# One-token attention with a gated MLP: five 32 KB slots and straight-line programs replaced by three 64 KB slots and a loop on each engine

## The chip, the core and the metric

The kernel runs on one core of a Trainium2 chip. The core's engines are TensorE (PE, matmuls; PEld is its weight load), VectorE (DVE), ScalarE (ACT), GpSimd (POOL) and SyncE (SP), which issues the transfers here; 16 DMA engines move data between HBM and the core's memory. The metric is the device time of one execution in microseconds, the median of several runs.

## The reference

For two rows of x (D = 448) the kernel computes one step of attention over a cache (16 heads of 256, 4096 cached positions), a ReLU MLP (1792 wide), and mixes the two by a sigmoid gate. All data is float32.

```python
q = (x @ wq).reshape(B, Sq, H, Dh)                      # B=2, Sq=1, H=16, Dh=256
scores = einsum("bhqd,bhkd->bhqk", q, k_cache) * Dh ** -0.5   # 4096 positions
o = einsum("bhqk,bhkd->bhqd", softmax(scores), v_cache)
a = o.reshape(B, Sq, H * Dh) @ wo
b = relu(x @ w1) @ w2
g = sigmoid((x * gate_w).sum(-1))
return g * a + (1 - g) * b
```

Keys and values are 134 MB each, the weights 21 MB. Each byte is used for one or two rows of x only.

## The kernel before

The work is cut into 32 units, one for each head and batch row (`U = 32`). A unit has 4 MB of keys (`kt[u]`, 128 partitions by 32 KB) and 4 MB of values (`vt[u]`). Each is one transfer of 128 rows of 32 KB into one of five slots of a ring (`SLOTS = 5`, `load`, L55), all of them issued by SP in program order. SP waits, before a transfer, until the slot's former content is used.

For each unit, `scores` runs 16 matmuls (32 passes in the trace, since each float32 matmul is two) on PE into one of two PSUM tiles `ps` (L153), DVE takes the maximum (L156), ACT the exponential with its sum (L158); `values` runs 8 products of the value slot with the probabilities on DVE, each with a running sum (L164). Positions are spread over four groups of 32 partitions; `combine` joins them with matmuls (L173 to L199), once for the first 16 units, in the middle of the program, and once for the last 16, at the end.

The query (`make_q`, L122 to L129) and the gate (`make_gate`) come first; x arrives in a small transfer of its own, issued by ACT. The hidden layer of the MLP (`hidden`, L211 to L224) runs in the middle, after unit 17. At the end come `mlp_out` (L238, 14 matmuls into `acc`) and the projection by `wo`: 26 of 32 slices into `acc` (L244), a copy (`a_sb`, L251), a matmul by `fold` that joins the four groups into `z` (L254), the last 6 slices straight into `z` (L258), the copy to `res` (L261) and the transfer of the result (L262). The second half of `wo` is loaded in four parts (L58):

```python
    CUTS = (0, NO - 10, NO - 6, NO - 2, NO)
    TAIL = 6
```

The order of the instructions on each engine is the order in which the code above is written out; the framework adds waits for buffers and data, and closes with a wait for all transfers, a barrier of all engines, the clearing of the semaphores and a second barrier (these stand under L342).

Of the kernel before, what the change touches and what calls it, by code (L numbers as in the profile page):

```python
# [1 line left out]

# [9 lines left out]
AX = mybir.AxisListType  # L12

P, HP = 128, 64
G = 4
R = P // G
SLOTS = 5
NB = 2


@with_exitstack
def tile_gated_mix_decode(ctx: ExitStack, tc: tile.TileContext, xg, kt, vt, wq, wo, w1, w2, out):
    nc = tc.nc
    U, _, T, S = kt.shape
    J, SG = vt.shape[2], vt.shape[3]
    KC, B = xg.shape[1], xg.shape[2] - 1
    KF = KC - 1
    NF, D = w2.shape[1], w2.shape[2]
    DG = D // G
    FG = NF * P // G  # L30
    H = U // B
    DH = T * P
    RB = R // B
    HB = H // NB
    UB = U // NB
    HH = HB // G
    CW = 512
    SCALE = float(DH) ** -0.5

    const = ctx.enter_context(tc.tile_pool(name="const", bufs=1))  # L40
    ring = ctx.enter_context(tc.tile_pool(name="ring", bufs=SLOTS))
    work = ctx.enter_context(tc.tile_pool(name="work", bufs=2))
    ps_s = ctx.enter_context(tc.tile_pool(name="ps_s", bufs=2, space=bass.MemoryType.PSUM))
    ps_w = ctx.enter_context(tc.tile_pool(name="ps_w", bufs=3, space=bass.MemoryType.PSUM))
    ps_a = ctx.enter_context(tc.tile_pool(name="ps_a", bufs=1, space=bass.MemoryType.PSUM))
    ctx.enter_context(tc.manual_schedule())

    def load(src, shape, cuts=None):
        t = ring.tile([P, T * S], F32, name="slot")
        n = 1  # L50
        for s in shape[1:]:
            n *= s
        flat = t[:, :n]
        if cuts is None:
            nc.sync.dma_start(flat, src)  # L55
        else:
            for lo, hi in zip(cuts, cuts[1:]):
                nc.sync.dma_start(flat[:, lo:hi], src[:, lo:hi])  # L58
        return t

    def psum(name="pw"):
        return ps_w.tile([P, CW], F32, name="pw")

    xg_sb = const.tile([P, KC, B + 1], F32, name="xg_sb")
    nc.scalar.dma_start(xg_sb, xg)
    wq_t = [load(wq[i], (P, wq.shape[2])) for i in range(NB)]

    ident = const.tile([P, P], F32, name="ident")
    make_identity(nc, ident)


    sel = const.tile([P, R], F32, name="sel")
    nc.vector.tensor_reduce(sel, ident.rearrange("p (g r) -> p r g", g=G), axis=AX.X, op=ALU.add)
    fsum = const.tile([P, B], F32, name="fsum")
    nc.vector.tensor_reduce(fsum, sel.rearrange("p (b r) -> p b r", b=B), axis=AX.X, op=ALU.add)
    fold = const.tile([P, B, RB], F32, name="fold")
    nc.vector.tensor_scalar(fold, fsum[:, :, None].to_broadcast([P, B, RB]), 1.0 / RB, None, op0=ALU.mult)


    xr = const.tile([P, KC, B, RB], F32, name="xr")  # L80
    nc.vector.tensor_copy(xr, xg_sb[:, :, :B, None].to_broadcast([P, KC, B, RB]))  # L81
    xu = const.tile([P, KC, UB // B, B], F32, name="xu")
    nc.vector.tensor_copy(xu, xg_sb[:, :, None, :B].to_broadcast([P, KC, UB // B, B]))

# [3 lines left out]
    def flat(a):  # L88
        return a.rearrange("p b r -> p (b r)")


    omg = const.tile([P, 1], F32, name="omg")
    gu = const.tile([UB, 1], F32, name="gu")

    def make_gate():
        pg = psum()
        for g in range(G):
            for c in range(KC):
                r = rows_of(c)
                nc.tensor.matmul(pg[g * R:(g + 1) * R, :1], flat(xr[r, c]), xg_sb[r, c, B:], start=(c == 0),  # L100
                                 stop=(c == KC - 1))
        gp = const.tile([P, 1], F32, name="gp")
        nc.scalar.activation(gp, pg[:, :1], AF.Sigmoid)
        nc.vector.tensor_scalar(omg, gp, -1.0, 1.0, op0=ALU.mult, op1=ALU.add)
        pu = psum()
        for c in range(KC):
            r = rows_of(c)
            nc.tensor.matmul(pu[:UB, :1], flat(xu[r, c]), xg_sb[r, c, B:], start=(c == 0), stop=(c == KC - 1))
        nc.scalar.activation(gu, pu[:UB, :1], AF.Sigmoid)


    qt = [const.tile([P, 2, T, G, B], F32, name=f"qt{i}") for i in range(NB)]
    W = 2 * KF * DH

    def make_q(i):
        pq = psum()
        w = wq_t[i]
        for c in range(KC):
            for g in range(G):
                r = rows_of(c, g // 2)  # L120
                at = g * W + c * CW if c < KF else G * W + g % 2 * CW
                nc.tensor.matmul(pq[g * R:(g + 1) * R, :], flat(xr[r, c]), w[r, at:at + CW], start=(c == 0),  # L122
                                 stop=(c == KC - 1))
        q = work.tile([P, CW], F32, name="q", bufs=1)
        nc.scalar.activation(q, pq, AF.Copy, scale=SCALE)
        pt = psum()
        for k in range(2 * T):
            nc.tensor.transpose(pt[:, k * P:(k + 1) * P], q[:, k * P:(k + 1) * P], ident)
        nc.scalar.activation(qt[i].rearrange("p s t g b -> p (s t g b)"), pt[:, ::RB], AF.Copy)  # L129

    nm = [const.tile([P, UB], F32, name=f"nm{i}") for i in range(NB)]
    ls = [const.tile([P, UB], F32, name=f"ls{i}") for i in range(NB)]
    ov = [const.tile([P, UB, J], F32, name=f"ov{i}") for i in range(NB)]
    junk = const.tile([P, SG], F32, name="junk")

    def place(u):
        h, b = divmod(u, B)
        i, hl = divmod(h, HB)  # L140
        hh, hq = divmod(hl, G)
        return i, (hq * HH + hh) * B + b

    def scores(u, k):
        h, b = divmod(u, B)
        i, at = place(u)
        hp, s = divmod(h % HB, 2)
        ps = ps_s.tile([P, SG], F32, name="ps")
        for c in range(SG // CW):
            for t in range(T):  # L150
                for g in range(G):
                    lo = t * S + g * SG + c * CW
                    nc.tensor.matmul(ps[g * R:(g + 1) * R, c * CW:(c + 1) * CW],  # L153
                                     qt[i][:, s, t, hp, b:b + 1].to_broadcast([P, R]), k[:, lo:lo + CW],
                                     start=(t == 0), stop=(t == T - 1))
        nc.vector.tensor_reduce(nm[i][:, at:at + 1], ps, axis=AX.X, op=ALU.max, negate=True)  # L156
        p = work.tile([P, SG], F32, name="p")
        nc.scalar.activation(p, ps, AF.Exp, bias=nm[i][:, at:at + 1], accum_out=ls[i][:, at:at + 1])  # L158
        return p

    def values(u, p, v):
        i, at = place(u)
        for j in range(J):
            nc.vector.scalar_tensor_tensor(junk, v[:, j * SG:(j + 1) * SG], 1.0, p, op0=ALU.mult, op1=ALU.mult,  # L164
                                           accum_out=ov[i][:, at, j:j + 1])

    acc = ps_a.tile([P, D], F32, name="acc")

    def combine(i):
        tp = psum()
        nc.tensor.transpose(tp[:UB, :P], nm[i], ident)  # L173
        nc.tensor.transpose(tp[:UB, P:2 * P], ls[i], ident)  # L174
        mt = tp[:UB, 0:P:R]
        lt = tp[:UB, P:2 * P:R]
        nb = work.tile([UB, 1], F32, name="nb")
        nc.vector.tensor_reduce(nb, mt, axis=AX.X, op=ALU.min)  # L178
        e = work.tile([UB, G], F32, name="e")
        nc.scalar.activation(e, mt, AF.Exp, bias=nb, scale=-1.0)  # L180
        el = work.tile([UB, G], F32, name="el")
        lsum = work.tile([UB, 1], F32, name="lsum")
        nc.vector.scalar_tensor_tensor(el, e, 1.0, lt, op0=ALU.mult, op1=ALU.mult, accum_out=lsum)
        rl = work.tile([UB, 1], F32, name="rl")
        nc.vector.reciprocal(rl, lsum)
        wb = work.tile([UB, G, R], F32, name="wb")
        nc.vector.tensor_scalar(wb, e[:, :, None].to_broadcast([UB, G, R]), rl, gu, op0=ALU.mult, op1=ALU.mult)  # L187
        wp = psum()
        nc.tensor.matmul(wp[:, :UB], wb.rearrange("u g r -> u (g r)"), ident[:UB, :UB], start=True, stop=True)  # L189
        os = work.tile([P, UB, J], F32, name="os", bufs=1)  # L190
        nc.vector.tensor_tensor(os, ov[i], wp[:, :UB, None].to_broadcast([P, UB, J]), op=ALU.mult)  # L191
        po = psum()
        n = HH * B * J
# [34 lines left out]

    NO = HH * J
    CUTS = (0, NO - 10, NO - 6, NO - 2, NO)
    TAIL = 6

# [112 lines left out]
```

## Time and profile before

| | us |
|---|---|
| median of three runs | 681.37 (681.27 to 681.67) |
| span of the profiled execution | 679.7 |
| DVE busy | 360.3 (53% of the span) |
| PE busy | 218.5 (32%) |
| ACT busy | 45.0 (7%) |

The span runs from the first instruction to the last; the profiled execution's own time is not printed beside its span, so that the median of the runs, 1.67 us above it, stands for it. The run has 289.55 MB of data transfers. The profile's rows give for each engine what it did, what it waited for, and how long; the windows query gives for any stretch the busy time of each engine, the share of time in which the 16 DMA engines were busy (1.00 is all of them) and the rate in GB/s.

### The profile page before, as it was taken

How to read it: one execution, taken by the hardware profiler on the slowest of the kernel's cores; microseconds unless marked ns; L12 is line 12 of the kernel's file. 1: busy time of each engine (PE TensorE's matmuls, PEld its weight loads, DVE VectorE, ACT ScalarE, POOL GpSimd, SP SyncE). 2: the span in 40 equal slices, each digit the busy share in tenths (PEclk: the TensorE clock that was granted, in tenths of full speed). 3: DMA queues.
4: the chain of work that ended last, by engine and by line, in shares of the span. 5: the costliest groups of instructions: out<-in, count | busy, mean ns of one | idle time of the engine just before them, and what ended most of it. 6: DMA issues, size and time to landing. Idle time of an engine off the chain costs nothing.

```text
span 679.7 us, 3604 instructions
## 1 busy us (share of the span) xinstructions
PE 218.5 (32%) x1335; PEld 58.7 (9%) x1335; DVE 360.3 (53%) x568; ACT 45.0 (7%) x78; POOL 0.7 (0%) x6
## 2 busy tenths in 40 slices
PE   2613333331223323322233152333322233333236
PEld 1100000000000000000000010000000000000002
DVE  0065555656655546566552738555656655556561
ACT  0100000000000000000000010000000000000000
POOL 0000000000000000000000000000000000000000
PEclk9876776656677676556765587666556676665568
DMA  9999999999999999999999999999999999999995
GB/s 377 429 434 432 434 437 434 432 434 434 435 434 432 434 431 432 432 432 432 431 435 433 429 431 434 432 432 433 432 434 432 434 433 432 432 436 435 436 421 236
DMA packets 10689, 289.77 MB, mean 426 GB/s; under 512 B 1328, under 2 KB 1328, under 8 KB 1712
## 3 DMA queue, kind: packets, MB, share of 16 engines
q1 hardware_dynamic: 10528, 289.55, 98.9%
q8 instruction: 10, 0.16, 0.1%
q14 instruction: 7, 0.06, 0.0%
q10 hardware_dynamic: 144, 0.01, 0.0%
HBM read 289.54 MB, written 0.00 MB: 426 GB/s over the span
## 4 chain that ended last, share of the span: by engine, by line
DMA 81%; DVE 11%; PE 7%; issue 0%; SPq 0%; ACT 0%; DVEq 0%
DMA slot<-in_vt 42%; DMA slot<-in_kt 33%; DVE junk L164 10%; DMA slot<-in_wo 6%; PE ps L153 5%; PE acc L244 1%; PE pw L211 1%; SPq L55 0%; PE pw L258 0%; DVE a_sb L251 0%; PE pw L189 0%; PE pw L254 0%; DVE wb L187 0%; PE pw L195 0%; DVE os L191 0%
## 5 line engine op out<-in xcount | busy, mean ns | idle before, releaser
L164 DVE SCALAR_TENSOR_TENSOR junk<-slot,p 128x1024 f32<-128x1024 f32 x256 | 313.5, 1225 | 88.5 <-DMA slot<-in_vt 79.4
L153 PE MATMUL ps<-slot,qt 128*32 128x512 f32 x1024 | 183.3, 881 | 414.6 <-DMA slot<-in_kt 414.6
L156 DVE TENSOR_REDUCE nm<-ps 128x1 f32<-128x1024 f32 x32 | 39.2, 1224 | 199.5 <-PE ps L153 199.5
L153 PEld LDWEIGHTS ps<-slot,qt 128*32 128x32 f32 x1024 | 45.6, 154 | 550.9 <-issue 524.4
L158 ACT ACTIVATE p<-ps,nm 128x1024 f32<-128x1024 f32 x32 | 35.6, 1113 | 562.0 <-DVE nm L156 562.0
L164 DVE DVE_READ_ACCUMULATOR junk<-slot,p 128x1 f32 x256 | 20.8, 81 | 0.0
L238 PE MATMUL acc<-slot,hr 128*32 128x448 f32 x28 | 5.6, 912 | 10.9 <-DMA slot<-in_w 10.9
L122 PE MATMUL pw<-slot,xr 128*32 128x512 f32 (+1 forms) x64 | 9.0, 700 | 0.0
L244 PE MATMUL acc<-slot,ot 128*32 128x448 f32 x52 | 7.1, 680 | 0.2 <-DMA slot<-in_wo 0.2
L100 PE MATMUL pw<-xg_sb,xr 128*32 128x1 f32 (+1 forms) x32 | 2.5, 196 | 12.6 <-DVE xr L81 12.6
L158 ACT ACTIVATION_READ_ACCUMULATOR p<-ps,nm 128x1 f32 x32 | 6.2, 193 | 0.0
L189 PE MATMUL pw<-ident,wb 16*128 16x16 f32 x4 | 1.0, 324 | 15.7 <-DVE wb L187 15.7
L81 DVE COPY xr<-xg_sb 128x128 f32<-128x128 f32 x1 | 0.2, 227 | 10.2 <-DMA xg_sb<-in_xg 10.2
L211 PE MATMUL pw<-slot,xr 128*32 128x448 f32 (+1 forms) x32 | 5.1, 782 | 0.0
L251 DVE COPY a_sb<-acc 128x448 f32<-128x448 f32 x1 | 0.6, 625 | 6.5 <-PE acc L244 6.5
L100 PEld LDWEIGHTS pw<-xg_sb,xr 128*32 128x32 f32 (+1 forms) x32 | 2.3, 147 | 12.7 <-DVE xr L81 12.6
L238 PEld LDWEIGHTS acc<-slot,hr 128*32 128x32 f32 x28 | 1.4, 166 | 15.2 <-DMA slot<-in_w 11.8
L244 PEld LDWEIGHTS acc<-slot,ot 128*32 128x32 f32 x52 | 2.0, 135 | 4.6 <-issue 4.1
L122 PEld LDWEIGHTS pw<-slot,xr 128*32 128x32 f32 (+1 forms) x64 | 1.9, 125 | 5.5 <-issue 5.5
L180 ACT ACTIVATE e<-pw,nb 16x4 f32<-16x4 f32 x2 | 0.5, 254 | 25.7 <-DVE nb L178 25.7
L189 PEld LDWEIGHTS pw<-ident,wb 16*128 16x128 f32 x4 | 0.8, 245 | 16.3 <-DVE wb L187 16.3
L178 DVE TENSOR_REDUCE nb<-pw 16x1 f32<-16x4 f32 x2 | 0.3, 148 | 3.3 <-PE pw L174 3.3
(46 smaller groups left out, 23.0 us busy)
## 6 DMA issues: line engine op xcount, KB each, us to landing
slot<-in_kt SPq DMA_DIRECT2D x32, 4096.0 KB, 38.2
slot<-in_vt SPq DMA_DIRECT2D x32, 4096.0 KB, 42.2
slot<-in_wq SPq DMA_DIRECT2D x2, 3584.0 KB, 11.3
slot<-in_w SPq DMA_DIRECT2D x2, 3136.0 KB, 36.4
slot<-in_wo SPq DMA_DIRECT2D x1, 3584.0 KB, 39.7
slot<-in_wo SPq DMA_DIRECT2D x2, 896.0 KB, 31.7
slot<-in_wo SPq DMA_DIRECT2D x1, 1344.0 KB, 29.2
slot<-in_wo SPq DMA_DIRECT2D x1, 448.0 KB, 33.1
```

The source lines that it names most:

```text
L100: nc.tensor.matmul(pg[g * R:(g + 1) * R, :1], flat(xr[r, c]), xg_sb[r, c, B:], start=(c == 0), stop=(c == KC - 1))
L122: nc.tensor.matmul(pq[g * R:(g + 1) * R, :], flat(xr[r, c]), w[r, at:at + CW], start=(c == 0), stop=(c == KC - 1))
L153: nc.tensor.matmul(ps[g * R:(g + 1) * R, c * CW:(c + 1) * CW], qt[i][:, s, t, hp, b:b + 1].to_broadcast([P, R]), k[:, lo:lo + CW], start=( ...
L156: nc.vector.tensor_reduce(nm[i][:, at:at + 1], ps, axis=AX.X, op=ALU.max, negate=True)
L158: nc.scalar.activation(p, ps, AF.Exp, bias=nm[i][:, at:at + 1], accum_out=ls[i][:, at:at + 1])
L164: nc.vector.scalar_tensor_tensor(junk, v[:, j * SG:(j + 1) * SG], 1.0, p, op0=ALU.mult, op1=ALU.mult, accum_out=ov[i][:, at, j:j + 1])
L180: nc.scalar.activation(e, mt, AF.Exp, bias=nb, scale=-1.0)
L189: nc.tensor.matmul(wp[:, :UB], wb.rearrange("u g r -> u (g r)"), ident[:UB, :UB], start=True, stop=True)
L211: nc.tensor.matmul(ph[g * R:(g + 1) * R, :FG], flat(xr[r, c]), w[r, at:at + FG], start=(c == 0), stop=(c == KC - 1))
L238: nc.tensor.matmul(acc[g * R:(g + 1) * R, :], hr[:, k, :], w[:, k * D:(k + 1) * D], start=(k < G), stop=False)
L244: nc.tensor.matmul(acc[g * R:(g + 1) * R, :], flat(ot[:, k // J, k % J]), w[:, k * D:(k + 1) * D], start=False, stop=(stop and k >= hi - G))
L251: nc.vector.tensor_copy(a_sb, acc)
```

## The change

The kernel is written anew without the framework, with its own semaphores.

- The program of each engine loops: PE, DVE and ACT run ten turns of three units each and two units behind the loop; SP runs nine turns of three transfers, with the transfers of the first and last units outside. A turn's waits compare semaphores with register values, and DVE, ACT and SP compute addresses in registers. No barrier stands in a loop.
- Keys and values of a unit are one array `kv`, 128 rows of 64 KB, one transfer into one of three slots of 64 KB. The last unit is split into keys and values. A slot comes free when DVE has done the unit's eight products (`freed`). These write over the values in place; there is no `junk` tile.
- One PSUM tile `sc` for the scores where there were two; PE starts a unit when ACT has done the exponential of the one before and has copied the unit's query (`queried`).
- x and the gate's weights ride in the rows of `wq`, which is one transfer; w1 and w2 are one transfer `wm` behind the last unit; `wo` is six transfers of 14, 9, 4, 2, 2 and 1 slices behind that.
- One `combine` for all 32 units. It and the hidden layer run at the end, behind `wm`, mixed with the 14 matmuls of the MLP's second layer. 23 slices of `wo` go into `acc`, 9 straight into `z`.
- The gate uses the exponential where there was a sigmoid. It is applied in `wb`, as before.
- The closing barrier and the clearing of the semaphores do not wait for the result's transfer; SP then waits for it and clears its semaphore.

```diff
-SLOTS = 5
-NB = 2
+SLOTS = 3
+CW = 512
+ACC = (14, 9)
+DIRECT = (4, 2, 2, 1)
+FOLD_AT = 1
...
+    slot = [nc.alloc_sbuf_tensor_at(f"slot{i}", [P, SW], F32, offset=first + i * SW * 4).ap() for i in range(SLOTS)]
...
+    sp.dma_start(slot[0][:, :wq.shape[1]], wq).then_inc(slot_in[0], 16)
+    sp.dma_start(slot[1], kv[0]).then_inc(slot_in[1], 16)
+    sp.dma_start(slot[2], kv[1]).then_inc(slot_in[2], 16)
...
+    def unit_pe(k, u_wait, slot_wait, s):
+        pe.wait_ge(slot_in[s], slot_wait)
+        pe.wait_ge(queried, u_wait)
         for c in range(SG // CW):
             for t in range(T):
                 for g in range(G):
                     lo = t * S + g * SG + c * CW
+                    m = pe.matmul(sc[g * R:(g + 1) * R, c * CW:(c + 1) * CW],
+                                  qc[:, s, t:t + 1].to_broadcast([P, R]), slot[s][:, lo:lo + CW],
+                                  start=(t == 0), stop=(t == T - 1))
+        m.then_inc(scored, 1)
+
+    def unit_act(u, u_wait, s, s_next, last=False):
+        act.wait_ge(maxed, u_wait)
+        act.activation(p, sc, AF.Exp, bias=nm[:, bass.ds(u, 1)], accum_out=ls[:, bass.ds(u, 1)]).then_inc(raised, 1)
+        if not last:
+            act.activation(qc[:, s_next, :], qt[:, bass.ds(u + 1, 1), :].rearrange("p o t -> p (o t)"),
+                           AF.Copy).then_inc(queried, 1)
+
+    def unit_dve(u, u_wait, s, v_sem=None):
+        dve.wait_ge(scored, u_wait)
+        dve.tensor_reduce(nm[:, bass.ds(u, 1)], sc, axis=AX.X, op=ALU.max, negate=True).then_inc(maxed, 1)
+        dve.wait_ge(raised, u_wait)
+        if v_sem is not None:
+            dve.wait_ge(v_sem, 16)
         for j in range(J):
+            v = slot[s][:, SW // 2 + j * SG:SW // 2 + (j + 1) * SG]
+            m = dve.scalar_tensor_tensor(v, v, 1.0, p, op0=ALU.mult, op1=ALU.mult,
+                                         accum_out=ov[:, bass.ds(u, 1), j].rearrange("p o -> p o"))
+        m.then_inc(freed, 1)
+
+    LOOP = (U - 2) // SLOTS
+    U1 = LOOP * SLOTS
...
+    w1 = slot[0][:, :W1]
+    w2 = slot[0][:, W1:W1 + NF * D]
+    w_o = slot[1]
...
+    with nc.Block(no_gpsimd_drain=True) as block:
+
+        @block.sync
+        def _(_e):
+            sp.wait_ge(q_mm, 2)
+            sp.dma_start(slot[0], kv[2]).then_inc(slot_in[0], 16)
+            with nc.Fori(0, LOOP - 1, engines=(ET.SP,)) as r:
+                u0 = sp.snap(r * SLOTS)
+                for k in range(SLOTS):
+                    s = (k + 1) % SLOTS
+                    sp.wait_ge(freed, u0 + k + 1)
+                    sp.dma_start(slot[s], kv[bass.ds(u0 + k + SLOTS, 1)].rearrange("o p n -> (o p) n")
+                                 ).then_inc(slot_in[s], 16)
+            sp.wait_ge(freed, U - 4)
+            sp.dma_start(slot[1], kv[U - 2]).then_inc(slot_in[1], 16)
+            sp.wait_ge(freed, U - 3)
+            sp.dma_start(slot[2][:, :SW // 2], kv[U - 1][:, :SW // 2]).then_inc(slot_in[2], 16)
+            sp.dma_start(slot[2][:, SW // 2:], kv[U - 1][:, SW // 2:]).then_inc(last_v, 16)
+            sp.wait_ge(freed, U - 2)
+            sp.dma_start(slot[0][:, :wm.shape[1]], wm).then_inc(mlp_in, 16)
+            sp.wait_ge(freed, U - 1)
+            k = 0
+            for n, s in zip(ACC + DIRECT, wo_in):
+                sp.dma_start(w_o[:, k * D:(k + n) * D], wo[:, k * D:(k + n) * D]).then_inc(s, 16)
+                k += n
+            sp.wait_ge(res_ok, 1)
+            sp.dma_start(out, res[0:7 * 15 + 1:7, :]).then_inc(out_sem, 16)
...
+            with nc.Fori(0, LOOP, 1, engines=(ET.PE,)) as r:
+                for k in range(SLOTS):
+                    s = (k + 1) % SLOTS
+                    unit_pe(k, r * SLOTS + (k + 1), r * 16 + (32 if s == 0 else 16), s)
+            for k in range(U - U1):
+                s = (k + 1) % SLOTS
+                unit_pe(k, U1 + k + 1, LOOP * 16 + 16, s)
...
+            pe.wait_ge(mlp_in, 16)
...
+            pe.wait_ge(freed, U)
+            pe.transpose(pc[:U, :P], nm, ident)
+            pe.transpose(pc[:U, P:2 * P], ls, ident).then_inc(ml_tr, 1)
+            pe.wait_ge(hr_ok, 1)
...
+            mlp(0, 4)
+            pe.wait_ge(wb_ok, 1)
+            pe.matmul(pa[:, :U], wb.rearrange("u g r -> u (g r)"), ident[:U, :U], start=True,
+                      stop=True).then_inc(wp_mm, 1)
+            mlp(4, 8)
+            pe.wait_ge(os_ok, 1)
...
+            mlp(8, NF)
+
+            def o_of(k):
+                return oc[:, k // J, k % J].rearrange("p r b -> p (r b)")
+
+            pe.wait_ge(oc_ok, 1)
+            k, n = 0, sum(ACC)
+            for i, a in enumerate(ACC):
+                pe.wait_ge(wo_in[i], 16)
+                for _ in range(a):
+                    g = k % G
+                    m = pe.matmul(acc[g * R:(g + 1) * R, :D], o_of(k), w_o[:, k * D:(k + 1) * D], start=False,
+                                  stop=(k >= n - G))
+                    k += 1
+            m.then_inc(acc_mm, 1)
+            for i, a in enumerate(DIRECT):
+                if i == FOLD_AT:
+                    pe.wait_ge(a_ok, 1)
+                    for g in range(G):
+                        pe.matmul(z[g * R:(g + 1) * R, :DG], fold.rearrange("p r b -> p (r b)"), a_sb[:, g * DG:(g + 1) * DG], start=False,
+                                  stop=False)
+                pe.wait_ge(wo_in[len(ACC) + i], 16)
+                for _ in range(a):
+                    for g in range(G):
+                        m = pe.matmul(z[g * R:(g + 1) * R, :DG], o_of(k),
+                                      w_o[:, k * D + g * DG:k * D + (g + 1) * DG], start=(k == n),
+                                      stop=(k == NO - 1))
+                    k += 1
+            m.then_inc(z_mm, 1)
...
+            with nc.Fori(0, LOOP, engines=(ET.DVE,)) as r:
+                u0 = dve.snap(r * SLOTS)
+                for k in range(SLOTS):
+                    u = dve.snap(u0 + k)
+                    unit_dve(u, u + 1, (k + 1) % SLOTS)
+            for u in range(U1, U):
+                unit_dve(u, u + 1, (u + 1) % SLOTS, last_v if u == U - 1 else None)
...
+    first_sem = min(s.num for s in sems)
+    last_sem = max(s.num for s in sems)
+    pool.sem_clear(range(first_sem, last_sem + 1))
+    sp.wait_ge(out_sem, 16)
+    sp.sem_clear(out_sem)
...
+    kv = np.concatenate([kt, vt], 2)
+    wq = np.concatenate([wq[0], wq[1], xg.reshape(P, -1)], 1)
+    arrays = {"wq": wq, "kv": kv, "wm": np.concatenate([w1, w2], 1), "wo": wo}
```

On SP (`slot_49`, `slot_50` and `slot_51` are the three slots), the end of the program before, from the last keys and values on:

```order
L55 DMA slot<-in_kt 128x8192
L55 DMA slot<-in_vt 128x8192
L55 DMA slot<-in_w 128x6272
L55 DMA slot<-in_wo 128x7168
L58 DMA slot<-in_wo 128x2688
L58 DMA slot<-in_wo 128x1792 x2
L58 DMA slot<-in_wo 128x896
L262 DMA out<-res 8x112
```

And the changed program's, from the last turn's branch on:

```order
L161 COMPARE_AND_BRANCH
L169 DMA slot_50<-in_kv 128x16384
L171 DMA slot_51<-in_kv 128x8192
L172 DMA slot_51<-in_kv 128x8192
L174 DMA slot_49<-in_wm 128x12544
L178 DMA slot_50<-in_wo 128x6272
L178 DMA slot_50<-in_wo 128x4032
L178 DMA slot_50<-in_wo 128x1792
L178 DMA slot_50<-in_wo 128x896 x2
L178 DMA slot_50<-in_wo 128x448
L181 DMA out<-res 16x112
```

Behind the last values the queue now holds w1 too, and the last part of `wo` is half as large; all of wo is cut where only its second half was.

On PE, the end of the program before, behind the last scores:

```order
L238 MATMUL acc<-slot,hr 32x448 x14
L173 MATMUL pw<-ident,nm_101 16x128
L174 MATMUL pw<-ident,ls_103 16x128
L189 MATMUL pw<-ident,wb 128x16
L195 MATMUL pw<-os,sel 32x32 x4
L244 MATMUL acc<-slot,ot 32x448 x26
L254 MATMUL pw<-a_sb,fold 32x112 x4
L258 MATMUL pw<-slot,ot 32x112 x24
```

And the changed program's, from the hidden layer's last rows on (L232 and L237, the rest of the hidden layer, stand ahead of them, behind the last scores; L243 to L261 are the combine, mixed with L250, the MLP's second layer):

```order
L239 MATMUL pb<-ident,hs 64x128 x2
L243 MATMUL pc<-ident,nm 32x128
L244 MATMUL pc<-ident,ls 32x128
L250 MATMUL acc<-slot_49,hr 32x448 x4
L255 MATMUL pa<-ident,wb 128x32
L250 MATMUL acc<-slot_49,hr 32x448 x4
L261 MATMUL pc<-os,sel 32x64 x4
L250 MATMUL acc<-slot_49,hr 32x448 x6
L275 MATMUL acc<-slot_50,oc 32x448 x23
L288 MATMUL z<-slot_50,oc 32x112 x16
L283 MATMUL z<-a_sb,fold 32x112 x4
L288 MATMUL z<-slot_50,oc 32x112 x20
```

The hidden layer has moved from the middle of the program to its end, the two combines have become one, and the fold stands between the slices that go straight into `z`, not ahead of them.

More of the change, by code (lines that the diff above doesn't have):

```diff
@@ L112, in tile_gated_mix_decode @@
[L112 to L129, printed above, removed]
@@ L133, in tile_gated_mix_decode, with x_of @@
[L133 to L148, printed above, removed]
+    def x_of(r, c, n=R):
+        return xr[r, c].rearrange("p r b -> p (r b)")[:, :n]
@@ L152, in scores @@
                     lo = t * S + g * SG + c * CW
[L153 to L158, printed above, removed]
@@ L159, in scores @@
-        return p
-    def values(u, p, v):
-        i, at = place(u)
-        for j in range(J):
[L164 to L193, printed above, removed]
-        for q in range(G):
-            nc.tensor.matmul(po[q * R:(q + 1) * R, :n], sel, os.rearrange("p u j -> p (u j)")[:, q * n:(q + 1) * n],
-                             start=True, stop=True)
-        ot = work.tile([P, HH, J, B, RB], F32, name="ot", bufs=NB)
-        for hh in range(HH):
-            nc.vector.tensor_copy(ot[:, hh], po[:, hh * B * J:(hh + 1) * B * J]
-                                  .rearrange("p (b j o) -> p j b o", j=J, o=1).to_broadcast([P, J, B, RB]))
-        return ot
@@ L247, in finish @@
-    def finish(ot, w):
-        n = NO - TAIL
-        project(ot, w, 0, n, True)
-        a_sb = const.tile([P, D], F32, name="a_sb")
-        nc.vector.tensor_copy(a_sb, acc)
-        z = psum()
-        for g in range(G):
-            nc.tensor.matmul(z[g * R:(g + 1) * R, :DG], flat(fold), a_sb[:, g * DG:(g + 1) * DG], start=True,
-                             stop=False)
-        for k in range(n, NO):
-            for g in range(G):
-                nc.tensor.matmul(z[g * R:(g + 1) * R, :DG], flat(ot[:, k // J, k % J]),
-                                 w[:, k * D + g * DG:k * D + (g + 1) * DG], start=False, stop=(k == NO - 1))
-        res = const.tile([P, DG], F32, name="res")
-        nc.vector.tensor_copy(res, z[:, :DG])
-        nc.sync.dma_start(out, res[::RB, :])
```

374 lines of the change are left out of this document (217 added, 157 removed).

## The prediction

> **What bounds the kernel now.** I read the page's span, its slices and its queues first.
>
> ```profile
> span 679.7 us, 3604 instructions
> PE 218.5 (32%) x1335; PEld 58.7 (9%) x1335; DVE 360.3 (53%) x568; ACT 45.0 (7%) x78; POOL 0.7 (0%) x6
> DMA  9999999999999999999999999999999999999995
> GB/s 377 429 434 432 434 437 434 432 434 434 435 434 432 434 431 432 432 432 432 431 435 433 429 431 434 432 432 433 432 434 432 434 433 432 432 436 435 436 421 236
> q1 hardware_dynamic: 10528, 289.55, 98.9%
> q8 instruction: 10, 0.16, 0.1%
> q14 instruction: 7, 0.06, 0.0%
> ```
>
> The DMA row is at 9 in every slice but the last, at 432 to 435 GB/s, while DVE, the busiest engine, works 53% of the span. 289.55 MB must be moved whatever the engines do; at 433 GB/s that is 668.7 us of the 679.7. So a change can only win at the two ends, in the rate, or in what else rides on the DMA engines: the instruction rows say that 17 transfers fetched program code.
>
> Next the windows query over the end of the stream (columns: stretch, length, busy time of the five engines, PE clock, DMA share, GB/s).
>
> ```profile
> 20.00:640.00 620.00, 189.80 (x1091) 48.23 (x1083) 344.25 (x534) 41.91 (x72) 0.00 (x0) 0.64 1.00 433
> 668.00:670.00 2.00, 2.00 (x14) 0.39 (x8) 0.00 (x0) 0.00 (x0) 0.00 (x0) 0.50 1.02 427
> 670.00:671.00 1.00, 1.00 (x16) 0.36 (x12) 0.00 (x0) 0.00 (x0) 0.00 (x0) 0.81 1.02 414
> 671.00:672.00 1.00, 1.00 (x16) 0.31 (x12) 0.00 (x0) 0.00 (x0) 0.00 (x0) 1.00 0.67 262
> 672.00:673.00 1.00, 1.00 (x16) 0.45 (x10) 0.00 (x0) 0.00 (x0) 0.00 (x0) 1.00 0.43 176
> 673.00:674.00 1.00, 1.00 (x10) 0.11 (x2) 0.00 (x0) 0.00 (x0) 0.00 (x0) 1.00 0.19 79
> 674.00:675.00 1.00, 0.18 (x6) 0.08 (x8) 0.62 (x1) 0.00 (x0) 0.00 (x0) 1.00 0.06 25
> 675.00:676.00 1.00, 1.00 (x45) 1.00 (x48) 0.00 (x0) 0.00 (x0) 0.00 (x0) 1.00 0.01 4
> ```
>
> The stream does not stop at once: it thins out from 671 on, and 0.06 (one engine of 16) is still busy after 674. The bytes after 670 are 414 + 262 + 176 + 79 + 25 + 4 = 960 KB, which all 16 engines together would have moved in 2.2 us, by 672.2. The last bytes come at about 675.2. So the uneven finish costs 3.0 us.
>
> Then the chain of waits at the end, the timeline's last DMA issue and SP's own waits.
>
> ```profile
> 667.04 7.12 PE acc L244 x52
> 674.18 0.64 DVE a_sb L251
> 674.95 0.40 PE pw L254 x8
> 675.35 1.18 PE pw L258 x48
> 676.55 0.27 DVE res L261
> 676.86 0.72 SPq L262 DMA_DIRECT2D out<-res  x1
> SPq L342 <- DMA out<-res: 1.0, 1, 1.0
> SPq L342 <- PEq L342: 0.6, 2, 0.4
> ```
>
> PE finishes at 676.5, 1.3 us behind the last bytes. The result is issued at 676.86 and is seen by SP at about 678.6 (0.72 of issue, 1.0 of wait); the 1.05 us from there to 679.7 is closing work at L342, in series.
>
> **The change, part by part.**
>
> *Looped programs: code fetches.* PE issued 1335 matmul passes and as many weight loads, 2670 instructions for 10 fetches on q8: one per 267. DVE's 568 and the few of ACT and SP made the 7 on q14. The new PE program is a loop body of 3 units (about 200 instructions) with some 720 around it, DVE's a body of about 85 with some 75 around it. If a loop is fetched once, about 3 + 1 transfers stay. Evenly spread, the 0.22 MB of code are 0.5 us of the stream: −0.5.
>
> *Looped programs: even finish.* Every data transfer gives each DMA engine the same share, so an engine that also carries code ends later. The 7 fetches of q14 are 0.06 MB, 2.2 us of one engine at 433/16 = 27 GB/s, if they all use one engine; a fetch of q8 is 0.6 us. That fits the one engine busy alone at 674 to 675, but no view names the engines. Bounds: 0 (the engines are uneven by themselves) to −3.0. The first to finish does so at about 671.0, 1.2 before the mean of 672.2; I let the last come half of that, 0.6, behind the mean: −2.4.
>
> *64 KB rows, fewer transfers.* Data rows fall from 9344 to 5248, and the 73 completions to 41 for each engine. No row separates what a packet costs. One end is 0; the other is that the 433 becomes the 435 of the better slices, 668.7 × 2/435 = −3.1. I take −1.0, nearer to 0, because the slice with w1's 25 KB rows (340 to 357 us: 435) reads no lower than its neighbours with 32 KB rows alone (431, 433). [...]
>
> *Three slots of 64 KB for five of 32 KB.* What could starve the stream is a slot that comes free late. From one unit of before, and below it the first and last step of q:
>
> ```profile
> 621.28 5.96 PE L153 MATMUL ps<-slot,qt 128*32 128x512 f32 x32 [13.98 <-DMA slot<-in_kt]
> 627.30 1.23 DVE L156 TENSOR_REDUCE nm<-ps 128x1 f32<-128x1024 f32 x1 [5.67 <-PE ps L153]
> 628.62 1.11 ACT L158 ACTIVATE p<-ps,nm 128x1024 f32<-128x1024 f32 x1 [18.73 <-DVE nm L156]
> 630.91 1.23 DVE L164 SCALAR_TENSOR_TENSOR junk<-slot,p 128x1024 f32<-128x1024 f32 x1 [2.38 <-DMA slot<-in_vt]
> 641.04 1.75 SPq L58 DMA_DIRECT2D slot<-in_wo  x4
> ...
> 15.36 5.27 PE L122 MATMUL pw<-slot,xr 128*32 128x512 f32 x32
> 27.25 0.20 ACT L129 ACTIVATE qt<-pw 128x32 f32<-128x32 f32 x1 [0.75 <-PE pw L128]
> ```
>
> Keys and values now land together, so the chain is 5.96 + 1.23 + 1.11 and its gaps (621.28 to 629.9) plus the 10.1 us of eight products (630.91 to 641.04): 18.8 us from landing to a free slot. A unit of 8.39 MB streams in 19.4 us, and two more are queued when one lands, 38.8 us of cover. 20 us are left, against register instructions, the single `sc` and the jumps back; SP's new wait on `freed` has only later transfers queued behind it, and they are not late before that is gone. Cost 0. The single `sc` makes PE wait for ACT's exponential, 8.6 us into a period of 19.4: covered too. At the start q needs all of wq (17 us) and then the 12.1 us of work from L122 to L129 (15.36 to 27.45); slot 0 is refilled at about 31, and wq, kv[0] and kv[1] last until about 58: 0. The x columns ride in wq: the 144-packet queue goes, 6 KB, 0.
>
> *The end on PE.* Hidden layer and both combines now come behind wm, with 7.34 MB of wo (17.0 us) still to stream. Rows for the moved work, from the middle of before and from its end:
>
> ```profile
> 390.36 5.07 PE L211 MATMUL pw<-slot,xr 128*32 128x448 f32 x32
> 395.50 0.63 ACT L214 ACTIVATE hs<-pw,omg 128x448 f32<-128x448 f32 x1 [7.05 <-PE pw L211]
> 396.19 0.55 PE L217 MATMUL pw<-ident,hs 128*128 128x128 f32 x3 [0.76 <-ACT hs L214]
> 397.15 0.49 ACT L221 ACTIVATE hr<-pw 128x384 f32<-128x384 f32 x1 [1.02 <-PE pw L219]
> 397.54 0.43 ACT L224 ACTIVATE hr<-pw 64x64 f32<-64x64 f32 x2
> 658.57 5.65 PE L238 MATMUL acc<-slot,hr 128*32 128x448 f32 x28 [10.94 <-DMA slot<-in_w]
> 664.57 0.15 DVE L178 TENSOR_REDUCE nb<-pw 16x1 f32<-16x4 f32 x1 [3.25 <-PE pw L174]
> 665.42 0.33 DVE L187 TENSOR_SCALAR wb<-e,rl,gu 16x128 f32<-16x128 f32 x1
> 666.92 0.76 DVE L199 COPY ot<-pw 128x256 f32<-128x256 f32 x2 [0.39 <-PE pw L195]
> ```
>
> L238 ran at the half clock: 0.20 us a pass. L244's 52 ran 3.4 us at that and then at full clock (0.50, then 0.81 and 1.00 in the windows): 17 passes, then 35 in 3.7 us, 0.106 each. Hidden 390.36 to 397.97 is 7.6 us. The combine (nb to wb, 664.57 to 665.75) starts about 0.4 before that and stands beside mlp(0,4), os beside mlp(4,8), and the four `oc` copies (4 × 0.38) beside mlp(8,14), about 0.5 longer than it. The 28 passes of mlp are 3.0 at full clock, the 46 of acc 4.9; 36 matmuls into z at L258's rate (24 in 1.18) 1.8, the fold 0.4; `a_sb` stands beside the first z part. Sum 18.2 after wm is seen, for a last part 17.0 behind it: PE ends about 1.5 us behind the last bytes, with 0.3 for how late a landing is seen, where it was 1.3: +0.2. Ends: 0.6 less (only the four matmuls of the last part), and +2.6 if mlp runs at the half clock, as L244's first passes did after three thin microseconds.
>
> *Closing.* The barrier and the clearing of semaphores run while the result leaves; behind its landing stands one clear. Of 1.05 I leave 0.2: −0.85.
>
> **The sum,** from the profiled execution's span of 679.7: −0.5 − 2.4 − 1.0 + 0.2 − 0.85 = −4.55, so 675.1. The median of the runs, 681.37, lies 1.67 above the span, and the profiled execution's own time is not given apart; I carry 1.67 over: 676.8, rounded to 676.7.
>
> **The rivals.**
>
> *Code is fetched again at each jump back (slower).* A loop body that lies across the edge of a fetched block would fetch on every turn, ten turns on DVE, always through the same queue. For it: 10 fetches for 2670 instructions show that PE gets code in blocks of about 260, and its body of 200 behind 175 others must cross an edge. Against: DVE's 85 are shorter than a block by any count (568 instructions, at most 7 fetches). Price of one fetch to the engine that carries it: 3.0 us of uneven finish over 7, 0.43 us. Two on each turn are 8.6 us, at the end of the stream in full: 676.7 + 8.6 = 685.3. It decides from 11 fetches on (4.7/0.43), a little over one on each turn. [...] Chance 0.16.
>
> *64 KB rows read worse (slower).* [...] Each 1% of rate costs 6.7 us, and it decides from 0.7% on: 1% gives 683.4. The rows with 32 KB are against it: 433 in the long window, 25 KB rows no different. [...] Chance 0.06.
>
> *The uneven finish stays.* If the engines are uneven by themselves, −2.4 falls away: 679.1. For it: no view ties fetches to the late engine. Chance 0.12.
>
> *The end on PE stays at the half clock:* 679.3. Chance 0.10. *Rows gain nothing,* or are still cut at 32 KB: 677.7. Chance 0.08.
>
> **How the numbers follow.** My forecast has 0.48, within 674.5 to 678.0 by its bounds (packets −2 more, PE −0.6; packets 0). The measurement tells about 0.2%, 1.4 us, from no change: faster is below 680.0. Forecast, PE clock, rows and most of the uneven finish are faster: 0.73; slower is both slower rivals less the few that stop short: 0.20; 0.07 between. The range must reach past the mild rivals: 674.5 to 682.5.
>
> **What the profile after would show.** Right: instruction rows with a handful of transfers; GB/s that falls from above 420 to nothing within 2 us; last bytes near 671; slices at 434 or more; PE done within 2 us of the last bytes; no idle slice in the middle; one short clear behind the result. Wrong: as many instruction transfers as before or more with one engine late at the end (first rival), slices below 430 all along (second), an uneven end without fetches (third).

## The result and the profile after

The changed kernel took 677.35 us (median of 4 runs, 676.62 to 677.45), the one before 681.32 on the same chip (681.16 to 681.67): a ratio of 0.9937, 95% interval 0.9923 to 0.9951. That is 0.63% faster. A second measurement, beside later experiments, gave 677.65 and 0.9947 [0.9933, 0.9960]. The profiled run of the changed kernel took 677.45.

The page's span, its engines, the GB/s row of the 40 slices, and the queues:

```profile
span 675.9 us, 3969 instructions
PE 211.9 (31%) x1309; PEld 52.0 (8%) x1309; DVE 340.4 (50%) x563; ACT 46.4 (7%) x107; POOL 0.7 (0%) x6
GB/s 380 434 431 435 431 434 434 434 434 434 434 434 434 434 434 434 434 434 434 434 434 434 434 434 434 434 434 434 434 434 434 434 434 434 434 434 431 449 407 275
q1 hardware_dynamic: 5936, 289.55, 99.1%
q8 instruction: 3, 0.05, 0.0%
q14 instruction: 1, 0.01, 0.0%
```

The program is still a stream: no slice in the middle falls, so three slots starve nothing. Data packets went from 10528 to 5936 and code transfers from 17 to 4. The GB/s row, which wandered between 429 and 437, now stands at 434 from the sixth slice to the thirty-sixth. The engines' work hardly changed (PE 218.5 to 211.9, DVE 360.3 to 340.4) and lies under the stream as it did.

The end of the stream (stretch, length, busy time of the five engines, PE clock, DMA share, GB/s):

```profile
669.00:670.00 1.00, 1.00 (x16) 0.33 (x12) 0.00 (x0) 0.00 (x0) 0.00 (x0) 1.00 0.99 393
670.00:671.00 1.00, 1.00 (x17) 0.33 (x12) 0.00 (x0) 0.00 (x0) 0.00 (x0) 1.00 0.29 104
671.00:672.00 1.00, 1.00 (x31) 0.69 (x27) 0.34 (x1) 0.00 (x0) 0.00 (x0) 1.00 0.06 22
```

Read as before: 393 + 104 + 22 = 519 KB are left at 669, which is 1.2 us for all engines, so an even finish would be at 670.2 (before: 672.2). The 22 KB of the last slice are 0.8 us of one engine at 27 GB/s, so the last bytes come at about 671.7 (before: 675.2). The uneven part has shrunk from 3.0 us to 1.5, not to the 0.6 forecast.

The trace also keeps a list of all DMA packets (start, length, size, queue), which the views shown here do not print. A packet carries no engine's name, but an engine's next packet starts where its last one ends, so that each engine's packets can be chained. This says what the 1.5 us are. Thirteen of the 16 engines are done by 670.3, the other three at 670.7, 671.4 and 671.6. Three code fetches come well ahead of the end, on three different engines: one of q14's 8 KB and two of PE's 16 KB. A fetch of 8 KB takes its engine 0.31 us, and the 64 KB packet behind it then takes 2.95 for 2.42: 0.84 in all. A fetch of 16 KB takes about 0.96 and makes the next packet 0.47 longer: 1.4 in all. At 630 us, ahead of the third fetch, the engines of the first two are 0.7 and 1.3 us behind the others, which fits the three late ends.

The chain of waits from `wm` on (start, length, what; times x2 and so on count instructions), its shortest pieces left out, then the last DMA issue in the timeline, and SP's wait for the result (total, times, longest):

```profile
618.61 36.30 DMA slot<-in_wm
654.96 5.42 PE pa L232 x32
660.40 0.64 ACT hs L315
661.09 0.55 PE pb L237 x3
662.05 0.49 ACT hr L317
...
662.64 0.23 ACTq L155
662.90 0.26 ACT e L325
...
663.56 0.34 DVE wb L358
663.95 0.40 PE pa L255 x2
664.36 0.89 PE acc L250 x8
665.42 1.43 DVE oc L363 x4
666.89 4.08 PE acc L275 x41
...
671.61 0.77 PE z L288 x30
672.37 0.37 PE z L283 x8
672.74 1.00 PE z L288 x40
673.77 0.28 DVE res L369
674.07 0.60 SPq L181 DMA_DIRECT2D out<-res  x1
SPq L375 <- DMA out<-res: 0.5, 1, 0.5
```

This chain hangs on `wm`, and no `wo` transfer stands in it: from 654.96 on PE and its helpers are never late because of `wo`. (The chain's 662.64 is the end of a piece; the timeline has the second copy into `hr` from 662.66 to 662.88, and PE starts `acc` L250 at 662.93.) PE ends at 673.74, 18.8 us behind the landing of `wm`, 2.0 behind the last bytes. From the result's issue at 674.07 it is 1.8 us to the end of the span; before it was 676.86 to 679.7, 2.8.

### The profile page after: what moved, and what is told of

Same layout as the page of the kernel before. It is cut to its first block, busy times and chain, and to the rows that moved or that the text cites. A ratio compares the mean times of both kernels' runs of the same rounds, so it can differ in the third digit from the quotient of the medians.

```text
span 675.9 us, 3969 instructions
## 1 busy us (share of the span) xinstructions
PE 211.9 (31%) x1309; PEld 52.0 (8%) x1309; DVE 340.4 (50%) x563; ACT 46.4 (7%) x107; POOL 0.7 (0%) x6
## 3 DMA queue, kind: packets, MB, share of 16 engines
q1 hardware_dynamic: 5936, 289.55, 99.1%
## 4 chain that ended last, share of the span: by engine, by line
DMA 69%; PE 12%; DVE 12%; issue 6%; DVEq 1%; ACT 1%; ACTq 0%; SPq 0%
DMA slot<-in_kv 61%; DVE slot L141 9%; PE sc L121 8%; DMA slot<-in_wm 5%; DMA slot<-in_wq 3%; DVE nm L135 2%; PE pb L206 1%; PE pa L232 1%; PE acc L275 1%; DVEq L141 1%; ACT p L128 0%; PE pa L195 0%; PE z L288 0%; DVE oc L363 0%; ACTq L307 0%
## 5 line engine op out<-in xcount | busy, mean ns | idle before, releaser
L141 DVE SCALAR_TENSOR_TENSOR slot<-slot,p 128x1024 f32<-128x1024 f32 x256 | 295.9, 1221 | 47.1 <-ACT p L128 47.1
L121 PE MATMUL sc<-slot,qc 128*32 128x512 f32 x1024 | 181.5, 874 | 419.4 <-DMA slot<-in_kv 419.4
L135 DVE TENSOR_REDUCE nm<-sc 128x1024 f32 (+1 forms) x32 | 39.2, 1225 | 243.9 <-PE sc L121 243.9
L121 PEld LDWEIGHTS sc<-slot,qc 128*32 128x32 f32 x1024 | 41.0, 153 | 559.2 <-issue 539.7
L128 ACT ACTIVATE p<-sc,nm 128x1024 f32<-128x1024 f32 x32 | 35.7, 1114 | 563.2 <-DVE nm L135 563.2
L141 DVE DVE_READ_ACCUMULATOR slot<-slot,p (+1 forms) x256 | 21.2, 83 | 0.0
L232 PE MATMUL pa<-slot,xr 128*32 128x448 f32 (+1 forms) x32 | 5.4, 826 | 18.7 <-DMA slot<-in_wm 18.7
L206 PE MATMUL pb<-slot,xr 128*32 128x512 f32 (+1 forms) x64 | 10.0, 763 | 0.0
L128 ACT ACTIVATION_READ_ACCUMULATOR p<-sc,nm (+1 forms) x32 | 6.2, 193 | 0.0
L130 ACT ACTIVATE qc<-qt 128x2 f32 (+1 forms) x31 | 6.0, 192 | 0.0
L250 PE MATMUL acc<-slot,hr 128*32 128x448 f32 x28 | 3.5, 546 | 0.6 <-ACT hr L320 0.6
L232 PEld LDWEIGHTS pa<-slot,xr 128*32 128x32 f32 (+1 forms) x32 | 1.1, 150 | 23.1 <-DMA slot<-in_wm 19.6
```

The lines of the kernel that those rows point to most:

```text
L121: m = pe.matmul(sc[g * R:(g + 1) * R, c * CW:(c + 1) * CW], qc[:, s, t:t + 1].to_broadcast([P, R]), slot[s][:, lo:lo + CW], start=(t == 0) ...
L128: act.activation(p, sc, AF.Exp, bias=nm[:, bass.ds(u, 1)], accum_out=ls[:, bass.ds(u, 1)]).then_inc(raised, 1)
L130: act.activation(qc[:, s_next, :], qt[:, bass.ds(u + 1, 1), :].rearrange("p o t -> p (o t)"), AF.Copy).then_inc(queried, 1)
L135: dve.tensor_reduce(nm[:, bass.ds(u, 1)], sc, axis=AX.X, op=ALU.max, negate=True).then_inc(maxed, 1)
L141: m = dve.scalar_tensor_tensor(v, v, 1.0, p, op0=ALU.mult, op1=ALU.mult, accum_out=ov[:, bass.ds(u, 1), j].rearrange("p o -> p o"))
L206: m = pe.matmul(pb[g * R:(g + 1) * R, :], x_of(r, c), w[r, at:at + CW], start=(c == 0), stop=(c == KC - 1))
```

## The experiments

The question was which part carries the 4 us, and why the refetching of looped code, the rival with the largest chance, did not come. A chip's measurement of one kernel moves by some 0.3 us from one comparison to the next (677.35 and 677.65 above), so where two intervals overlap the landing of `wm` and the last bytes in the traces decide.

**All loops written out.** All four engines' loops become straight programs; one of the four, for the others alike:

```diff
-            with nc.Fori(0, LOOP, engines=(ET.DVE,)) as r:
-                u0 = dve.snap(r * SLOTS)
+            for r in range(LOOP):
+                u0 = r * SLOTS
```

> The changed kernel with all four loops written out as straight-line programs, everything else kept. Theory (code fetches, and above all DVE's, which ride on one DMA engine): about 10 fetches on q8 and 5 to 7 on q14 come back, one engine ends the stream some 2 to 3 us later, last bytes at about 674 instead of 671.6, time 679.0 to 680.0 against the changed kernel's 677.35. Rival (the engines are uneven by themselves, code is only bytes): 0.2 MB more over 16 engines, at most 0.4 us, time 677.4 to 677.8.

678.91 (678.00 to 679.43), ratio 0.9965 [0.9951, 0.9978]: 1.3 to 1.6 above the changed kernel. The profiled run is its fastest, 0.9 below its median. Queues and the landing of `wm`:

```profile
q8 instruction: 10, 0.16, 0.1%
q14 instruction: 5, 0.04, 0.0%
656.19 4.74 PE pa L231 x32
```

The fetches are back, `wm` is seen at 656.19 for 654.96, 1.2 later. By the packet list the last bytes come at 672.95, 1.3 later, where 2 to 3 were expected, and the time lies just under the expected range. About a third of the gain is the loops.

**DVE's loop alone written out** (the diff above and nothing else).

> Only DVE's loop is written out. Theory (DVE's fetches share one engine, about 0.5 us each): 5 fetches on q14 where there was 1, last bytes 1.7 to 2.1 us later, time 679.0 to 679.5, nearly all of what writing out all loops costs. Rival 1 (PE's many fetches made the late engine): no change, 677.3 to 677.5. Rival 2 (uneven by themselves): the same 677.4.

678.61 (678.38 to 679.08), 0.9961 [0.9948, 0.9975]. The queue, the landing, and the end of the stream:

```profile
q14 instruction: 4, 0.03, 0.0%
656.51 4.79 PE pa L232 x32
672.00:673.00 1.00, 1.00 (x34) 0.75 (x30) 0.41 (x1) 0.00 (x0) 0.00 (x0) 1.00 0.07 27
673.00:674.00 1.00, 1.00 (x45) 0.79 (x39) 0.21 (x1) 0.00 (x0) 0.00 (x0) 1.00 0.01 5
```

Three fetches more, 0.02 MB in all, and `wm` is seen 1.55 later, the last bytes come at about 673.2 for 671.7: 0.5 us for a fetch. Spread over 16 engines 0.02 MB would be 0.05 us. The slice at 0.07 says who pays: one engine of 16 still at work, at one engine's 27 GB/s. The packet list ties DVE's fetches to it: all four lie on one engine, which is 3.1 us behind the others at 600 us. In the changed kernel this queue's engine was the one done at 670.7; three fetches more at 0.84 each make 673.2. The end moved by less than these 2.5 us because there another engine, with one of PE's fetches, was the last. The time, 678.61, lies under the expected 679.0 to 679.5.

**PE's loop alone written out.**

```diff
-            with nc.Fori(0, LOOP, 1, engines=(ET.PE,)) as r:
+            for r in range(LOOP):
```

> Only PE's loop is written out. Theory (PE's fetches go to a different DMA engine each time): 10 fetches on q8 where there were 3, but the last engine only 0 to 0.9 us later, time 677.3 to 678.3. Rival (they add up on one engine): 7 more at about 0.5 us, 680.5 to 681.

678.94 (677.92 to 679.24), 0.9957 [0.9943, 0.9970]. A miss: more than expected.

```profile
q8 instruction: 10, 0.16, 0.1%
656.04 6.11 PE pa L232 x32
671.00:672.00 1.00, 1.00 (x16) 0.33 (x12) 0.00 (x0) 0.00 (x0) 0.00 (x0) 1.00 0.22 79
672.00:673.00 1.00, 1.00 (x16) 0.40 (x11) 0.00 (x0) 0.00 (x0) 0.00 (x0) 1.00 0.05 18
```

Seven fetches more put `wm` 1.1 later, and the last bytes come at about 672.7, 1.0 later. The theory's mechanism holds all the same: in the packet list the eight fetches of PE ahead of 600 us lie on eight different engines, each 1.4 us on its own. The ninth, at 634.5, falls on an engine that has had one, and this engine ends last, at 672.7; most of the other engines with a fetch end at about 671.3, so that at 671 to 672 several are still at work (a share of 0.22), where DVE's fetches left one. The first product behind `wm` then took 6.11 for 5.42, and this 0.7 is PE's clock, not the fetches: behind the product's start the granted clock stayed at 0.50 for about 5.6 us here, for 4.1 in the changed kernel and for 2.8 with all loops written out, where the same 32 passes took 4.74. With DVE's 1.55 and PE's 1.1 apart but 1.2 for both together, the two do not add: with all loops written out the two last engines end at 672.7 and 672.95, and the later one counts.

**Rows of 32 KB.** Each unit is two transfers again, keys and values, in the same slot (the loop's part is shown; the transfers outside it are split alike, and PE waits for both):

```diff
-                    sp.dma_start(slot[s], kv[bass.ds(u0 + k + SLOTS, 1)].rearrange("o p n -> (o p) n")
-                                 ).then_inc(slot_in[s], 16)
+                    row = kv[bass.ds(u0 + k + SLOTS, 1)].rearrange("o p n -> (o p) n")
+                    sp.dma_start(slot[s][:, :SW // 2], row[:, :SW // 2]).then_inc(slot_in[s], 16)
+                    sp.dma_start(slot[s][:, SW // 2:], row[:, SW // 2:]).then_inc(slot_in[s], 16)
```

> Each unit comes as two transfers with 32 KB rows (keys, values) into the same 64 KB slot, waited for together; loops and all else kept. Theory (a packet has a fixed cost of about 4 ns, so half as many packets gave the sum's -1.0): the whole stream ends 0.8 to 1.4 us later on all engines, time 678.1 to 678.8. [...]

678.30 (677.88 to 678.59), 0.9953 [0.9939, 0.9967].

```profile
q1 hardware_dynamic: 10400, 289.56, 99.2%
655.93 5.27 PE pa L236 x32
672.00:673.00 1.00, 1.00 (x36) 0.70 (x28) 0.51 (x1) 0.00 (x0) 0.00 (x0) 1.00 0.07 25
```

`wm` is seen 0.97 later, and by the packet list the last bytes come at 672.6, 1.0 later. The intervals of the times overlap; the landings agree with a packet's price: 4464 packets more over 16 engines are 279 each, 3.5 ns apiece. The packet list shows the price itself: an engine starts a 64 KB packet every 2.414 us and a 32 KB packet every 1.209, so that two halves take 4 ns more than the whole.

**The changed kernel again, and its barrier behind the result.** SP waits for the result's landing ahead of the closing barrier, as the kernel before did:

```diff
             sp.dma_start(out, res[0:7 * 15 + 1:7, :]).then_inc(out_sem, 16)
+            sp.wait_ge(out_sem, 16)
...
-    sp.wait_ge(out_sem, 16)
     sp.sem_clear(out_sem)
```

> The changed kernel itself once more, as the yardstick for the runs beside it. Both theories: 677.3, between 676.6 and 677.5.

> SP waits for the result's landing ahead of the closing barrier, not behind it; all else kept. Theory (the closing work was hidden behind the result): barrier and clear come back in series, 0.5 to 0.85 us more, time 677.8 to 678.2. Rival (what follows the last instruction waits for the same thing anyway): within 0.2 of the changed kernel.

677.65 (677.40 to 678.11) and 678.26 (677.48 to 678.97), ratios 0.9947 [0.9933, 0.9960] and 0.9952 [0.9939, 0.9966]. Of the second the page's span, the chain's last PE piece, and SP's wait:

```profile
span 676.4 us, 3970 instructions
672.63 1.00 PE z L289 x40
SPq L155 <- DMA out<-res: 1.1, 1, 1.1
```

From PE's end to the span's end it is 2.8 us (673.63 to 676.4), for 2.2 (673.74 to 675.9) in the changed kernel: 0.6 for the order of the closing. The times, 0.6 apart, overlap; the span of one execution of each is what shows it.

**`wm` in two transfers.** If the chain hangs on one 6.4 MB landing that holds w1 and w2, w1 should come with a semaphore of its own:

```diff
-            sp.dma_start(slot[0][:, :wm.shape[1]], wm).then_inc(mlp_in, 16)
+            sp.dma_start(slot[0][:, :W1], wm[:, :W1]).then_inc(w1_in, 16)
+            sp.dma_start(slot[0][:, W1:wm.shape[1]], wm[:, W1:]).then_inc(mlp_in, 16)
...
-            pe.wait_ge(mlp_in, 16)
+            pe.wait_ge(w1_in, 16)
...
+            pe.wait_ge(mlp_in, 16)
             mlp(0, 4)
```

> wm comes as two transfers, w1 and then w2, so that the hidden layer starts some 7 us earlier; the order on PE and all bytes are kept. Theory (the end is PE's chain from the landing of wm on, 18.8 us against 17 us of stream, not the last bytes): PE ends about 0.8 us behind the last bytes instead of 2.1, 0.9 to 1.4 us less, time 675.9 to 676.5. Rival (PE waits for the last part of wo anyway): within 0.2 of the changed kernel.

676.32 (675.94 to 676.43), 0.9924 [0.9911, 0.9938]: 1.3 below the changed kernel's 677.65 in the same comparison, with no run in common. The chain of waits and the stream's last slice:

```profile
637.19 25.00 DMA slot<-in_wo
662.33 7.22 PE acc L277 x45
...
671.29 1.00 PE z L290 x24
671.00:672.00 1.00, 0.98 (x36) 0.53 (x28) 0.00 (x0) 0.00 (x0) 0.00 (x0) 1.00 0.06 22
```

The last bytes stand where they stood, about 671.7; the hidden layer and the combine have gone under the stream, `wo` takes the place of `wm` in the chain, and PE ends at 672.29, 0.6 behind the last bytes for 2.0. This version beats both kernels.

**A long DVE body, and a middle one.** The loop body of DVE becomes 15 units (some 410 instructions, two turns), and in a later kernel 6 units (some 165, five turns), for 3 (83, ten turns). The edit of the first:

```diff
-            with nc.Fori(0, LOOP, engines=(ET.DVE,)) as r:
-                u0 = dve.snap(r * SLOTS)
-                for k in range(SLOTS):
+            with nc.Fori(0, 2, engines=(ET.DVE,)) as r:
+                u0 = dve.snap(r * 15)
+                for k in range(15):
```

> DVE's loop takes 15 units in a turn (two turns), a body of some 415 instructions, where it was 3 units and 83; the other engines keep theirs. [...] Rival (code once fetched stays, whatever the length): 4 fetches as with the loop written out, 678.4 to 679.0.

> DVE's loop with a body of 6 units (166 instructions) and five turns, for 3 units (83) and ten; the work is the same. [...]

The long body: 683.81 (683.13 to 684.78), ratio 1.0039 [1.0025, 1.0052], slower than the kernel before. The middle one: 676.91 (676.50 to 677.40), 0.9933 [0.9920, 0.9947], as the changed kernel, with 2 fetches on q14. The long body's queue, and its stream's end:

```profile
q14 instruction: 9, 0.07, 0.0%
674.00:675.00 1.00, 1.00 (x16) 0.39 (x12) 0.00 (x0) 0.00 (x0) 0.00 (x0) 1.00 0.06 25
...
677.00:678.00 1.00, 1.00 (x33) 0.70 (x27) 0.62 (x1) 0.00 (x0) 0.00 (x0) 1.00 0.05 18
```

The same work, as a loop, fetches 9 times where the straight program fetched 4: its second turn fetches the body again (the jump back is at 323.3, and five fetches start between 328.8 and 562). One engine is alone at work from 674 to about 677.7, 6.0 us later than in the changed kernel. In the packet list all nine fetches lie on this engine, and the eight ahead of 600 us cost it 0.84 to 0.97 us each: 0.31 for the fetch and 0.53 to 0.66 more for the 64 KB packet behind it. At 600 us it is 6.8 us behind the others. In the changed kernel the engine of this queue was done at 670.7, so that eight fetches more moved it by 7.0, 0.87 each. At the 0.5 us a fetch expected for DVE's loop alone they would have been 4.0. The middle body, like the changed kernel's, is not fetched again on each of its turns (2 fetches, five turns).

**Three parts undone at once**: loops written out, 32 KB rows, the barrier behind the result, by the diffs above.

> All four loops written out, units as two transfers of 32 KB rows, and SP waiting for the result ahead of the barrier: three parts of the change undone at once; the three slots, the joined wm, the cut of wo and the closing clear stay as changed. Theory (the three parts act one after the other on the end of the stream and so add): 677.5 + 1.3 (loops alone) + 0.95 (rows alone) + 0.6 (closing alone) = 680.3, 680.0 to 680.7, last bytes 2.2 later than in the changed kernel, at about 673.8. Rival (fetches and rows cost the same latest engine only once): 679.2 to 679.6. Rival (the three are all of the change): 681.2 to 681.6.

681.23 (680.50 to 681.86) beside 681.50 for the kernel before (681.08 to 681.76): ratio 0.9996 [0.9987, 1.0005]. Queues, landing, end of PE:

```profile
q1 hardware_dynamic: 10400, 289.56, 98.9%
q8 instruction: 10, 0.16, 0.1%
q14 instruction: 5, 0.04, 0.0%
657.65 5.27 PE pa L237 x32
675.28 1.00 PE z L293 x40
```

The rival is right: these three are the whole gain, to within the interval (0.9 us faster to 0.3 slower than the kernel before). What stays of the change (three slots, one joined combine, `wm` and the cut of `wo`, single buffers) is, taken together, worth nothing that can be measured. Part by part it need not be nothing: by the run with `wm` in two, its joining alone costs 1.3. One at a time the three gave 1.3 to 1.6, about 1.0 and 0.6, some 3.0 in all, for 4.2 together (the changed kernel did not run in this comparison; its two other kernels ran at 676.9 and 677.0). The traces place part of the rest: `wm` is seen 2.7 later for 1.2 + 1.0, and PE's end to the span's end is 3.0 for 2.8. Why is open.

**`wo` cut as before** (`ACC = (16, 6, 4)`, `DIRECT = (4, 2)` for `(14, 9)` and `(4, 2, 2, 1)`).

> wo in five parts that end where those of the kernel before did (16, 6, 4, then 4 and 2 straight into z) for six (14, 9, then 4, 2, 2, 1); nothing else changed. Theory (PE is late at the end by its own work behind wm, not by the last part): 677.2 to 677.9, PE still about 2 us behind the last bytes. Rival (the finer cut is the rest of the gain that the other three parts leave): 678.2 to 678.8.

676.99 (676.58 to 678.26), 0.9937 [0.9924, 0.9951]: no difference from the changed kernel, as the theory had it. While PE is late by its own work behind `wm`, the size of the last part of `wo` does not count.

## Why the prediction was right, and where its terms were off

The forecast was 676.7 (its own sum gives 676.8); the median is 677.35, the span 675.9 for 675.1. The likeliest case came, and the 0.8 us splits into terms. Some of them are off in opposite directions, so that the sum is nearer than its parts.

- *Code fetches.* About 3 + 1 transfers were to stay; q8 has 3 and q14 has 1. Right.
- *Even finish.* The last bytes were to come at about 671.3 and came at 671.7. The mechanism is shown: three DVE fetches move the end by 1.55, and in the packet list of the kernel before, five of q14's seven fetches lie on one engine, the last to end, while of `wm`'s 128 packets in the changed kernel each engine has eight. But the uneven rest is 1.5 us, not 0.6, and the even finish came at 670.2, 0.5 earlier than summed. "I let the last come half of that behind the mean" was a guess with no row under it; what is left is the full price of one of PE's fetches on its engine. The prices were too low: 0.43 us for a fetch of q14, taken from 3.0 over 7, is 0.84 on its engine, and 0.6 for one of PE's is 1.4. That the end still came near 671.3 is in part luck: an even finish 0.5 too late and a rest 0.9 too small.
- *64 KB rows.* Forecast 1.0 at the lower part of 0 to 3.1; undoing them cost 0.97 at the landing of `wm`. Right. With 64 KB rows the slices stand at 434, where they lay between 429 and 437.
- *Three slots, single `sc`.* Cost 0; no slice falls between 20 and 640 us. Right.
- *The end on PE.* This step failed in size. 18.2 us behind `wm` became 18.8, and 1.5 behind the last bytes became 2.0. The 0.3 for how late a landing is seen was the author's estimate, with no row beside it; in the packet list the last packet of `wm` ends at 654.51, and PE starts at 654.96, 0.45 later. The hidden layer took 8.0 (654.96 to 662.93, where PE goes on; summed 7.6); its first product alone took 5.42 for the row's 5.07, with the clock at 0.50 for 4.1 us. `acc` from 666.89 to 671.61 took 4.7 (4.9), `z` with the fold 2.1 (2.2). The most mis-sized term is the combine with `mlp`: from 662.93 to 666.89 it took 4.0 for 3.5. The prediction let the combine stand beside `mlp` and left its own matmuls on PE out of the sum; in the chain they are 0.40 (L255) and 0.16 (L261). The wait for `wb` is not what it costs: ACT's `e` does stand behind `hr` in ACT's program, and `wb` is done only at 663.89, but until then PE is at work on `mlp(0, 4)`, and L255 starts 0.06 later. That PE was late at all was not costed as a chance to gain; the split of `wm` shows that it was worth 1.3.
- *Closing.* 0.85 was forecast, with 0.2 left behind the landing, an estimate under which no row stands. The time from issue to the end fell from 2.8 to 1.8, 1.0; putting the wait back gave 0.6 of it, alone, and PE's end to the span's end was 3.0 with all three parts undone. Right in direction, between 0.6 and 1.0 in size.
- *The rivals.* Refetching did not come: one fetch on q14 in ten turns. But it does happen, and its price was about half of what was measured (0.43 for 0.84 or more). A body of some 410 instructions was fetched again (9 fetches on q14) and ran slower than the kernel before; 83 (1) and some 165 (2) were not. DVE's fetches are 8 KB each in the packet list. Whether DVE waits for them is not shown here, and no length between 165 and 410 was run. Rows of 64 KB read no worse (434), the uneven finish did shrink, and PE's clock, at 0.50 under the hidden layer's first product until about 659, was at 1.00 from 660 to the end, so under `mlp`, which that rival had priced.

## What to carry to other kernels

When DMA is busy from end to end, look at what rides on it besides data and at the last slices of the stream: three 8 KB code fetches cost 1.5 us because one engine of 16 carried them and everyone waits for the last one. Here a loop took them away while its body was small (some 165 instructions did, some 410 turned the gain of 4 us into a loss of 2.5). And what is joined into one landing starts as one: joining w1 and w2 put 18.8 us of work behind the later one, and a transfer and a semaphore for each gave 1.3 us back.

## What the runs showed that was not expected

- A code fetch cost its engine more than its own time. A fetch of 8 KB took 0.31 us, which is 27 GB/s, but the 64 KB packet behind it took 0.53 longer. Why is not shown.
- PE's fetches are 16 KB and cost their engine 1.4 us, DVE's are 8 KB and cost 0.84, yet seven of PE's moved the landing of `wm` by 1.1 and three of DVE's by 1.55: the first eight of PE's went to eight different engines, all of DVE's to the same one.
- The same 32 passes of the hidden layer, at the same place, took from 4.74 to 6.11 us between kernels that differ only elsewhere. The time goes with how long the granted clock stays at 0.50 behind their start: 2.8 us in the one and 5.6 in the other. What sets that is not shown.
